# Swapping which half of the split weights takes the recycled slots, and a new order of the first loads, in an attention and rational-gate kernel

## The chip, the cores and the metric

The kernel runs on one core of one Trainium2 chip. The metric is device time in microseconds (us). The engines are PE (matrix products and transposes), DVE, ACT and POOL (elementwise work), and SP, which here only issues DMAs; ACT can issue DMAs too. Each engine takes its instructions in a fixed order and waits at the one whose inputs are not ready.

## The reference

```python
# attention, q k v of shape (4, 8, 768, 64), 8 global keys, a local window of 96
scores = q @ k.T / sqrt(D)  -  slope[h] * distance
scores = where(is_global | is_local, scores, -1e9)
a = softmax(scores)
x = (a @ v)  as (3072, 512)
# feed-forward, w_in (512, 2048), w_out (2048, 512)
h = x @ w_in
P = a[0] + a[1]*h + a[2]*h**2 + a[3]*h**3
Q = 1 + |b[0]|*|h| + |b[1]|*h**2
out = (P / (Q + 1e-6)) @ w_out
```

`moe_w_in` and `moe_w_out` arrive as 64-bit floats. The kernel fetches their raw words and puts them together to 32-bit floats itself.

## The kernel before

**Tiling.** The 3072 rows are 12 chunks of 256 tokens. A chunk has 8 attention units (a unit u is a pair of heads for 128 tokens; 96 units) and 8 feed-forward steps (a step f covers 256 of the 2048 hidden columns; 96 steps). A step's first layer gives h (L277, for chunk 0 L269), a gate of elementwise work follows, and the second layer adds to the chunk's output (L353, for chunk 0 L348). The gate runs over ACT (L301 to L303, logarithm and exponential L317 and L318), DVE (L308, L309, then L322 to L324, whose last instruction ends the gate) and POOL (the sum L310). From chunk 1 on ACT and POOL also split the gate's result into two parts (L332, L333).

**Two kinds of products.** Chunk 0 multiplies in full 32 bits with the decoded weights. From chunk 1 on (step 8), every operand is split into a high part, rounded to the type fp32r, and a low part, the difference; three fp32r products (high by high, high by low, low by high) take the place of one.

**The weights** come in 32 pieces of 128x512: `w_in` piece (1, row block, column block), `w_out` piece (0, row block). `WSCHED` says at which time step which pieces are decoded, beginning with the four of the first column block of `w_in`. A piece is fetched (L177, 512 KB, into one of five raw buffers), decoded on ACT or POOL (L206 to L212) and on DVE (L213, then L215, which ends it) into a full piece, named `w..f`. `first` holds the first five pieces, fetched by `windowed` at the start; each later fetch waits for a raw buffer that a decode leaves. Later `split_w` makes the parts: the copy L228 rounds (DVE and ACT by turns, `HI_V`), the subtraction L229 takes the difference (POOL, from the 14th piece on by turns with DVE, `LO_V`). `SPLITS` sets after which step which pieces are split, in the order of their decoding.

**Places.** High parts lie in two fixed tiles, `win_h` and `wout_h`. Full pieces and low parts share the pool `lows`: 33 slots in rotation. The full pieces come first in it (the first two parts ahead of the last two), so low part n + 1 lands in the slot that full piece n had: the subtraction waits until that piece has been split and read for the last time by chunk 0. The copy writes a fixed place and waits for the decode of its piece alone.

**What sets the order.** Every instruction gets a priority (`tc.cur_priority`, from the time step and the tables `PRI` and `PRI_A`), and a scheduler builds the order of each engine from the priorities, the dependencies and its own times. Splitting (`wsplit`) has the lowest priority, so a copy that is ready is put where an engine would stand idle.

**The start.** SP issues the two flag DMAs (`n_local`, `n_global`, needed by the masks), then q and k of the first units (`st_load(0)`), q and k of the next (`st_load(2)`), V (`st_load_v`), and the remaining fetches. ACT loads its table and issues the first two pieces.

Of the kernel before, what the change touches and what calls it, by code (L numbers as in the profile page):

```python
# [105 lines left out]
def tile_kernel(ctx: ExitStack, tc: tile.TileContext, q, k, v, n_global, n_local,  # L106
# [28 lines left out]
    def st_load(u):  # L135
        c, t, p, b, i = unit(u)
        hs = slice(2 * p, 2 * p + 4)
        r = slice(i * P, (i + 1) * P)
        n = pl.ldp.tile([P, 2, 4, D], F32, tag="nat", name=f"nat{u}")
        nc.sync.dma_start(out=n[:, 0], in_=q[b, hs, r, :].rearrange("h s d -> s h d"))  # L140
        nc.sync.dma_start(out=n[:, 1], in_=k[b, hs, r, :].rearrange("h s d -> s h d"))
        nat[u // 2] = n
# [4 lines left out]
        nc.sync.dma_start(out=vt, in_=v[b, 2 * p:2 * p + 4, i * P:(i + 1) * P, :].rearrange("h s d -> s h d"))  # L147


    win_h = const.tile([P, NCT, DF], FR, name="win_h")  # L150
    wout_h = const.tile([P, NFT, DM], FR, name="wout_h")
    lows = ctx.enter_context(tc.tile_pool(name="lows", bufs=1))
    full = {}
    low = {}

    def piece(dt, key):
        return lows.tile([P, 2 * TOK], dt, tag="w", name=f"w{'_'.join(map(str, key))}{'f' if dt is F32 else 'l'}",
                         bufs=NCT * DF // (2 * TOK) + NFT + 1)

    def w_hi(key):  # L160
        if key[0]:
            return win_h[:, key[1], key[2] * 2 * TOK:(key[2] + 1) * 2 * TOK]
        return wout_h[:, key[1], :]

    def tmp(name):
        return pl.ffn.tile([P, 2, TOK], F32, tag="tmp", name=name, bufs=pl.tmps)
# [57 lines left out]
        return [(0, 2 * n + x) for x in range(2)]  # L224

    def split_w(key):
        low[key] = piece(FR, key)
        (nc.vector.tensor_copy if len(low) - 1 in HI_V else nc.scalar.copy)(out=w_hi(key), in_=full[key])  # L228
        (nc.vector if len(low) - 1 in LO_V else nc.gpsimd).tensor_tensor(  # L229
            out=low[key], in0=full[key], in1=w_hi(key), op=ALU.subtract)  # L230


    gs = {}
# [27 lines left out]
    def st_ffn1(f, y):  # L261
        c, j = divmod(f, FPC)
        if y == 0:
            hps[f] = pl.ps_h.tile(sh, F32, tag="h", name=f"h{f}")
        jw, fw = divmod((2 * j + y) * P, 2 * TOK)
        fs = slice(fw, fw + P)
        if c == 0 and not pl.split:
            for ct in range(NCT):
                nc.tensor.matmul(out=hps[f][:, y, :], lhsT=full[1, ct, jw][:, fs], rhs=xT[c][:, ct, :],  # L269
                                 start=(ct == 0), stop=(ct == NCT - 1))  # L270
            return
        xh, xl = xT[c]
        n = 0
        for ct in range(NCT):
            wh, wl = w_hi((1, ct, jw)), low[1, ct, jw]
            for w, x in ((wh, xh), (wh, xl), (wl, xh)):
                nc.tensor.matmul(out=hps[f][:, y, :], lhsT=w[:, fs], rhs=x[:, ct, :],  # L277
                                 start=(n == 0), stop=(n == 3 * NCT - 1))
                n += 1
# [59 lines left out]
    def st_ffn2(f, t):  # L339
        c, j = divmod(f, FPC)  # L340
        if j == 0:
            accs[c, t] = pl.ps_o.tile([P, DM], F32, tag="acc", name=f"acc{c}_{t}")
        acc = accs[c, t]
        ts = slice(t * P, (t + 1) * P)
        for y in range(2):
            ft = 2 * j + y
            if c == 0 and not pl.split:
                nc.tensor.matmul(out=acc, lhsT=gs[f][:, y, ts], rhs=full[0, ft],  # L348
                                 start=(ft == 0), stop=(ft == NFT - 1))
                continue  # L350
            wh = w_hi((0, ft))
            for n, (z, w) in enumerate(((0, wh), (0, low[0, ft]), (1, wh))):
                nc.tensor.matmul(out=acc, lhsT=gs[f][:, z, y, ts], rhs=w,  # L353
                                 start=(ft == 0 and n == 0), stop=(ft == NFT - 1 and n == 2))
        if j == FPC - 1:
            o = tmp(f"o{c}_{t}").rearrange("p a b -> p (a b)")
            rows = slice(c * TOK + t * P, c * TOK + (t + 1) * P)
            if is_last(f):
                (nc.vector.tensor_copy if t else nc.scalar.copy)(out=o, in_=acc)
            else:  # L360
                nc.any.tensor_copy(out=o, in_=acc)
            nc.sync.dma_start(out=out[rows, :], in_=o)
# [187 lines left out]
    nf = const.tile([P, 4], F32, name="nf")  # L550

    def windowed(lates):
        nc.sync.dma_start(out=ni[:, 0:2], in_=n_local.bitcast(I32).partition_broadcast(P))
        nc.sync.dma_start(out=ni[:, 2:4], in_=n_global.bitcast(I32).partition_broadcast(P))
        first = [key for t in sorted(WSCHED) for kind, j in WSCHED[t] for key in pieces(kind, j)][0:GBUFS + 2]
        scope = ExitStack()
        pl.early = scope.enter_context(tc.tile_pool(name="early", bufs=1))
        pl.kF = pl.early.tile([P, NPAIR, 2, P], F32, name="kF")
        pl.kGF = pl.early.tile([P, NPAIR, G], F32, name="kGF")
        pl.qz = pl.early.tile([P, 3, 2, P], F32, name="qz")  # L560
        nc.scalar.preload_act_table_set("natural_log_exp_and_others")
        st_load(0)
        for n, key in enumerate(first):
            fetch(key, nc.scalar if n < 2 else nc.sync)
            if n == 0:
                st_load(2)
                st_load_v(0)
                st_load_v(2)
        make_identity(nc, ident)
# [244 lines left out]
```

## Time and profile before

| | us |
|---|---|
| median of three runs | 784.45 |
| the three runs | 784.35, 784.45, 787.12 |
| the profiled execution, its own time | 783.55 |
| its span, first to last instruction | 781.5 |
| PE busy | 748.3 |
| granted clock of PE, mean | 0.992 |

All times of the profile are counted from the first instruction. Busy time is the sum over an engine's instructions, overlaps within it taken once; idle time matters only where the engine is what the others wait for. In group names the numbers of buffers are left out: `w_10f` is a full piece, `w_3l` a low part, `nat` holds q and k of two units, `fu` is the operand that the gate gives to the second layer.

### The profile page before, as it was taken

What the parts mean: (1) busy time and instruction counts of PE and PEld (TensorE: products, weight loads), DVE (VectorE), ACT (ScalarE), POOL (GpSimd) and SP (SyncE); (2) the same over time, 40 slices, a digit from 0 to 9 for tenths busy, and PEclk for the clock granted to TensorE, in tenths of its full rate; (3) what the DMA queues carried; (4) which work ended last, traced back from release to release, by engine and by line L of the source; (5) the groups of instructions that cost most, each with busy time, mean ns of one, the idle gap of its engine ahead of it and who ended that gap; (6) DMA issues with size and microseconds to landing.
All of it is one profiled execution on the core that took longest, in us unless ns stands there. A gap on an engine that the chain in (4) does not pass through costs nothing.

```text
span 781.5 us, 15335 instructions
## 1 busy us (share of the span) xinstructions
PE 748.3 (96%) x5216; PEld 648.6 (83%) x5216; DVE 567.6 (73%) x1384; ACT 571.7 (73%) x1404; POOL 501.3 (64%) x548
## 2 busy tenths in 40 slices
PE   3798799999999999999999999999999999999996
PEld 2575466888988988998998998989988989988995
DVE  5899987656677777776776767776776776776665
ACT  4798755876786777877776877777777777776764
POOL 4675785355687686676677676675676677664441
PEclk9999899999999999999999999999999999999999
DMA  8886300202322212222212222222222221100000
GB/s 225 269 265 211 97 16 13 63 22 58 79 49 49 73 44 49 67 51 62 60 43 49 65 52 49 63 56 55 62 48 49 62 56 44 41 22 1 28 1 33
DMA packets 97560, 52.75 MB, mean 68 GB/s; under 512 B 81088, under 2 KB 90304, under 8 KB 97472
## 3 DMA queue, kind: packets, MB, share of 16 engines
q1 hardware_dynamic: 97184, 50.62, 24.6%
q10 hardware_dynamic: 288, 1.05, 0.4%
q8 instruction: 44, 0.72, 0.4%
q14 instruction: 44, 0.36, 0.2%
HBM read 35.92 MB, written 6.29 MB: 54 GB/s over the span
## 4 chain that ended last, share of the span: by engine, by line
PE 88%; DVE 5%; ACT 3%; issue 1%; DMA 1%; POOL 0%; SPq 0%; DVEq 0%; ACTq 0%
PE h L277 33%; PE acc L353 32%; PE o L519 5%; PE s L449 4%; PE tp L497 4%; PE acc L348 3%; PE tk L403 3%; PE h L269 2%; PE s L444 1%; DVE r L213 1%; DMA nat<-in_k_dram 1%; ACT pr L473 1%; PE tk L396 0%; ACT qz L418 0%; DVE w_0f L215 0%
## 5 line engine op out<-in xcount | busy, mean ns | idle before, releaser
L353 PE MATMUL acc<-wout_h,g 128*128 128x512 f32 x704 | 249.3, 405 | 0.0
L277 PE MATMUL h<-xh,win_h 128*128 128x256 f32 x704 | 205.3, 292 | 0.0
L277 PE MATMUL h<-xl,win_h 128*128 128x256 f32 x704 | 197.5, 281 | 0.0
L310 POOL TENSOR_TENSOR fa<-fa,fs 128x512 f32<-128x512 f32 x95 | 124.1, 1306 | 97.1 <-ACT fs L303 93.7
L487 POOL TENSOR_SCALAR pr<-pr,stats 128x256 f32<-128x256 f32 (+1 forms) x152 | 131.4, 875 | 36.9 <-DVE stats L478 26.2
L353 PEld LDWEIGHTS acc<-wout_h,g 128*128 128x128 f32 x704 | 128.8, 188 | 22.0 <-ACT g L332 0.4
L277 PEld LDWEIGHTS h<-xh,win_h 128*128 128x128 f32 x704 | 132.9, 189 | 7.4 <-issue 5.8
L277 PEld LDWEIGHTS h<-xl,win_h 128*128 128x128 f32 x704 | 132.4, 188 | 1.6 <-issue 0.3
L473 ACT ACTIVATE pr<-pr,stats 128x256 f32<-128x256 f32 (+1 forms) x192 | 92.6, 484 | 53.3 <-DVE stats L463 53.2
L333 POOL TENSOR_TENSOR g<-fu,g 128x512 fp32r<-128x512 f32 x87 | 112.6, 1295 | 8.7 <-ACT g L332 6.1
L301 ACT ACTIVATE fu<-h,coef 128x512 f32<-128x512 f32 (+1 forms) x97 | 75.0, 773 | 57.5 <-PE h L277 52.5
L322 DVE SCALAR_TENSOR_TENSOR fu<-fu,coef,q 128x512 f32<-128x512 f32 (+1 forms) x97 | 71.7, 739 | 46.0 <-ACT q L318 45.1
L387 POOL TENSOR_TENSOR sp<-nat,sp 128x256 fp32r<-128x256 f32 x72 | 53.0, 736 | 78.7 <-DVE sp L386 36.7
L317 ACT ACTIVATE fs<-fa,coef 128x512 f32<-128x512 f32 (+1 forms) x97 | 69.6, 717 | 34.3 <-POOL fa L310 33.1
L499 DVE COPY pT<-tp 128x512 f32<-128x512 f32 (+1 forms) x75 | 48.5, 646 | 53.4 <-PE tp L497 52.4
L308 DVE TENSOR_TENSOR fu<-fu,h 128x512 f32<-128x512 f32 (+1 forms) x97 | 65.5, 675 | 19.9 <-ACT fs L303 18.1
L309 DVE SCALAR_TENSOR_TENSOR fu<-fu,coef,h 128x512 f32<-128x512 f32 (+1 forms) x97 | 71.8, 740 | 2.7
L323 DVE SCALAR_TENSOR_TENSOR q<-fa,coef,q 128x512 f32<-128x512 f32 (+1 forms) x97 | 72.1, 743 | 0.0
L463 DVE CUSTOM_DVE_ANT_0 pr<-s,masks 128x256 f32<-128x256 f32 x160 | 61.1, 418 | 11.2 <-PE s L444 5.3
L302 ACT ACTIVATE fa<-h,coef 128x512 f32<-128x512 f32 (+1 forms) x97 | 65.6, 676 | 2.0 <-DVE q L323 1.0
L303 ACT ACTIVATE fs<-h,coef 128x512 f32<-128x512 f32 (+1 forms) x97 | 66.4, 684 | 0.1
L324 DVE SCALAR_TENSOR_TENSOR fu<-q,fu 128x512 f32<-128x512 f32 (+1 forms) x97 | 65.7, 677 | 0.4
(247 smaller groups left out, 1636.3 us busy)
## 6 DMA issues: line engine op xcount, KB each, us to landing
qT<-qT SPq DMA_DIRECT2D x144, 64.0 KB, 2.0
r<-in_moe_w_out_dram SPq DMA_DIRECT2D x16, 512.0 KB, 4.9
r<-in_moe_w_in_dram SPq DMA_DIRECT2D x14, 512.0 KB, 4.6
nat<-in_q_dram SPq DMA_DIRECT2D x48, 128.0 KB, 2.7
nat<-in_k_dram SPq DMA_DIRECT2D x48, 128.0 KB, 2.6
vt<-in_v_dram SPq DMA_DIRECT2D x48, 128.0 KB, 2.4
out_dram<-o SPq DMA_DIRECT2D x24, 256.0 KB, 2.1
r<-in_moe_w_in_dram ACTq DMA_DIRECT2D x2, 512.0 KB, 7.1
```

The costliest lines, as they stand in the source:

```text
L277: nc.tensor.matmul(out=hps[f][:, y, :], lhsT=w[:, fs], rhs=x[:, ct, :], start=(n == 0), stop=(n == 3 * NCT - 1))
L301: nc.scalar.activation(out=u, in_=h, func=AF.Identity, scale=a3, bias=a2)
L303: nc.scalar.activation(out=s, in_=h, func=AF.Square, scale=b1)
L309: nc.vector.scalar_tensor_tensor(out=u, in0=u, scalar=a1, in1=h, op0=ALU.add, op1=ALU.mult)
L310: side(f).tensor_tensor(out=a, in0=a, in1=s, op=ALU.add)
L317: nc.scalar.activation(out=s, in_=a, func=AF.Ln, bias=q1)
L322: nc.vector.scalar_tensor_tensor(out=u, in0=u, scalar=a0, in1=r, op0=ALU.add, op1=ALU.mult)
L323: nc.vector.scalar_tensor_tensor(out=r, in0=a, scalar=q1, in1=r, op0=ALU.add, op1=ALU.mult)
L333: side(f).tensor_tensor(out=g[:, 1, ys], in0=u, in1=g[:, 0, ys], op=ALU.subtract)
L353: nc.tensor.matmul(out=acc, lhsT=gs[f][:, z, y, ts], rhs=w, start=(ft == 0 and n == 0), stop=(ft == NFT - 1 and n == 2))
L473: nc.scalar.activation(out=d, in_=d, func=AF.Exp, scale=-1.0, bias=st[:, x:x + 1], accum_out=st[:, 2 + 2 * x:3 + 2 * x])
L487: nc.gpsimd.tensor_scalar(out=d, in0=d, scalar1=st[:, 6 + x:7 + x], scalar2=None, op0=ALU.mult)
```

## The change

The pool now holds full pieces and high parts (`wide`); the fixed tiles hold the low parts (`win_l`, `wout_l`). Sizes and the rotation stay as they are, and so do all operations and their engines: the copy writes a slot and the subtraction a fixed place. The three products read the same operands from the swapped places.

At the start the two flag DMAs go from SP to ACT, ahead of its table load. SP begins with q and k of the first units, then the first piece, q and k of the next units, the second and third piece, V, and the rest. ACT issues no fetch any more.

```diff
-    win_h = const.tile([P, NCT, DF], FR, name="win_h")
-    wout_h = const.tile([P, NFT, DM], FR, name="wout_h")
-    lows = ctx.enter_context(tc.tile_pool(name="lows", bufs=1))
+    win_l = const.tile([P, NCT, DF], FR, name="win_l")
+    wout_l = const.tile([P, NFT, DM], FR, name="wout_l")
+    wide = ctx.enter_context(tc.tile_pool(name="wide", bufs=1))
...
     def split_w(key):
-        low[key] = piece(FR, key)
-        (nc.vector.tensor_copy if len(low) - 1 in HI_V else nc.scalar.copy)(out=w_hi(key), in_=full[key])
-        (nc.vector if len(low) - 1 in LO_V else nc.gpsimd).tensor_tensor(
-            out=low[key], in0=full[key], in1=w_hi(key), op=ALU.subtract)
+        hi[key] = piece(FR, key)
+        (nc.vector.tensor_copy if len(hi) - 1 in HI_V else nc.scalar.copy)(out=hi[key], in_=full[key])
+        (nc.vector if len(hi) - 1 in LO_V else nc.gpsimd).tensor_tensor(
+            out=w_lo(key), in0=full[key], in1=hi[key], op=ALU.subtract)
...
-            wh, wl = w_hi((1, ct, jw)), low[1, ct, jw]
+            wh, wl = hi[1, ct, jw], w_lo((1, ct, jw))
...
-            wh = w_hi((0, ft))
-            for n, (z, w) in enumerate(((0, wh), (0, low[0, ft]), (1, wh))):
+            wh = hi[0, ft]
+            for n, (z, w) in enumerate(((0, wh), (0, w_lo((0, ft))), (1, wh))):
...
     def windowed(lates):
-        nc.sync.dma_start(out=ni[:, 0:2], in_=n_local.bitcast(I32).partition_broadcast(P))
-        nc.sync.dma_start(out=ni[:, 2:4], in_=n_global.bitcast(I32).partition_broadcast(P))
...
+        nc.scalar.dma_start(out=ni[:, 0:2], in_=n_local.bitcast(I32).partition_broadcast(P))
+        nc.scalar.dma_start(out=ni[:, 2:4], in_=n_global.bitcast(I32).partition_broadcast(P))
+        st_load(0)
         nc.scalar.preload_act_table_set("natural_log_exp_and_others")
-        st_load(0)
         for n, key in enumerate(first):
-            fetch(key, nc.scalar if n < 2 else nc.sync)
-            if n == 0:
+            if n == 1:
                 st_load(2)
+            fetch(key)
+            if n == 2:
                 st_load_v(0)
                 st_load_v(2)
```

The line numbers behind the start move by one.

The first place is SP at the start of the program (`r1_2_0` is the raw buffer of piece (1, 2, 0), `vt` holds V). Before, where two pieces more stand on ACT's queue:

```order
L553 DMA ni_69<-in_n_local_dram 128x2
L554 DMA ni_69<-in_n_global_dram 128x2
L140 DMA nat0_101<-in_q_dram 128x4x64
L141 DMA nat0_101<-in_k_dram 128x4x64
L140 DMA nat2_106<-in_q_dram 128x4x64
L141 DMA nat2_106<-in_k_dram 128x4x64
L147 DMA vt0_109<-in_v_dram 128x4x64
L147 DMA vt2_111<-in_v_dram 128x4x64
L177 DMA r1_0_0_115<-in_moe_w_in_dram 128x1024
L177 DMA r1_1_0_117<-in_moe_w_in_dram 128x1024
L177 DMA r1_2_1_119<-in_moe_w_in_dram 128x1024
```

And now:

```order
L140 DMA nat0_100<-in_q_dram 128x4x64
L141 DMA nat0_100<-in_k_dram 128x4x64
L177 DMA r1_2_0_104<-in_moe_w_in_dram 128x1024
L140 DMA nat2_106<-in_q_dram 128x4x64
L141 DMA nat2_106<-in_k_dram 128x4x64
L177 DMA r1_3_0_109<-in_moe_w_in_dram 128x1024
L177 DMA r1_0_0_111<-in_moe_w_in_dram 128x1024
L147 DMA vt0_113<-in_v_dram 128x4x64
L147 DMA vt2_115<-in_v_dram 128x4x64
L177 DMA r1_1_0_117<-in_moe_w_in_dram 128x1024
L177 DMA r1_2_1_119<-in_moe_w_in_dram 128x1024
```

q and k of the first units have moved to the front of SP, the first two pieces have joined it, and V has moved behind the third piece.

The second place is DVE near the end of the decoding, around the last instruction of step 2's gate (L324 with `fu2`; the ISA rows are the masked scores of L463). Before:

```order
L308 TENSOR_TENSOR fu3_811<-fu3_811,h3_793 128x512
L215 SCALAR_TENSOR_TENSOR w0_11f_931<-w0_11f_931,r0_11_932 128x512
L463 ISA pr14_942,stats_64<-s14_938,masks_68 128x256
L463 ISA stats_64 128x1
L463 ISA pr14_942,stats_64<-s14_938,masks_68 128x256
L463 ISA stats_64 128x1
L546 TENSOR_TENSOR xl1_675<-o5_834,xh1_674 128x2x128
L228 CAST wout_h_59<-w0_10f_924 128x512
L215 SCALAR_TENSOR_TENSOR w0_13f_1016<-w0_13f_1016,r0_13_1017 128x512
L213 SCALAR_TENSOR_TENSOR r0_14_1087<-r0_14_1087 128x512
L324 SCALAR_TENSOR_TENSOR fu2_729<-q2_804,fu2_729 128x512
L228 CAST wout_h_59<-w0_12f_1009 128x512
```

And now, where the copy L228 that follows is the first one on DVE:

```order
L213 SCALAR_TENSOR_TENSOR r0_12_1010<-r0_12_1010 128x512
L215 SCALAR_TENSOR_TENSOR w1_3_3f_860<-w1_3_3f_860,r1_3_3_861 128x512
L476 TENSOR_REDUCE stats_64<-stats_64 128x2
L546 TENSOR_TENSOR xl1_675<-o5_834,xh1_674 128x2x128
L324 SCALAR_TENSOR_TENSOR fu2_729<-q2_804,fu2_729 128x512
L213 SCALAR_TENSOR_TENSOR r0_11_932<-r0_11_932 128x512
L215 SCALAR_TENSOR_TENSOR w0_10f_924<-w0_10f_924,r0_10_925 128x512
L309 SCALAR_TENSOR_TENSOR fu3_811<-fu3_811,coef_63,h3_793 128x512
L228 CAST w1_2_0h_1023<-w1_2_0f_174 128x512
L215 SCALAR_TENSOR_TENSOR w0_12f_1009<-w0_12f_1009,r0_12_1010 128x512
L213 SCALAR_TENSOR_TENSOR r0_13_1017<-r0_13_1017 128x512
L478 RECIPROCAL stats_64<-stats_64 128x2
```

Before, fourteen copies of DVE stand ahead of this L324; now none does, and the last steps of the decodes of `w0_10` to `w0_13` stand behind it.

The third place is POOL where the first layer of chunk 1 gets its weights (L229 writes the low part; the gate's sum L310 between them belongs to steps 4 to 7). Before, a subtraction reads a full piece and the fixed tile, and writes a slot:

```order
L229 TENSOR_TENSOR w1_2_1l_1177<-w1_2_1f_272,win_h_58 128x512
L229 TENSOR_TENSOR w1_3_1l_1180<-w1_3_1f_277,win_h_58 128x512
L310 TENSOR_TENSOR fa4_902<-fa4_902,fs4_903 128x512
L229 TENSOR_TENSOR w1_0_1l_1183<-w1_0_1f_310,win_h_58 128x512
L229 TENSOR_TENSOR w1_1_1l_1186<-w1_1_1f_317,win_h_58 128x512
L229 TENSOR_TENSOR w0_0l_1262<-w0_0f_386,wout_h_59 128x512
L229 TENSOR_TENSOR w0_1l_1265<-w0_1f_393,wout_h_59 128x512
```

And now it reads a full piece and the slot of its high part:

```order
L229 TENSOR_TENSOR win_l_58<-w1_2_1f_272,w1_2_1h_1177 128x512
L229 TENSOR_TENSOR win_l_58<-w1_3_1f_277,w1_3_1h_1180 128x512
L451 COPY kF_95<-kGF_96 128x8
L229 TENSOR_TENSOR win_l_58<-w1_0_1f_310,w1_0_1h_1183 128x512
L310 TENSOR_TENSOR fa6_1064<-fa6_1064,fs6_1065 128x512
L229 TENSOR_TENSOR win_l_58<-w1_1_1f_317,w1_1_1h_1186 128x512
L229 TENSOR_TENSOR wout_l_59<-w0_0f_386,w0_0h_1262 128x512
L229 TENSOR_TENSOR wout_l_59<-w0_1f_393,w0_1h_1265 128x512
```

The same subtractions stand about one and a half steps later among the gates' sums. Copy n + 1 writes the slot of full piece n, which subtraction n reads, so before each subtraction a copy on DVE or ACT has to have run that waited for the subtraction before it.

More of the change, by code (lines that the diff above doesn't have):

```diff
@@ L147, in st_load_v, with w_lo @@
         nc.sync.dma_start(out=vt, in_=v[b, 2 * p:2 * p + 4, i * P:(i + 1) * P, :].rearrange("h s d -> s h d"))
-    win_h = const.tile([P, NCT, DF], FR, name="win_h")
-    wout_h = const.tile([P, NFT, DM], FR, name="wout_h")
-    lows = ctx.enter_context(tc.tile_pool(name="lows", bufs=1))
+    win_l = const.tile([P, NCT, DF], FR, name="win_l")
+    wout_l = const.tile([P, NFT, DM], FR, name="wout_l")
+    wide = ctx.enter_context(tc.tile_pool(name="wide", bufs=1))
     full = {}
-    low = {}
+    hi = {}
     def piece(dt, key):
-        return lows.tile([P, 2 * TOK], dt, tag="w", name=f"w{'_'.join(map(str, key))}{'f' if dt is F32 else 'l'}",
+        return wide.tile([P, 2 * TOK], dt, tag="w", name=f"w{'_'.join(map(str, key))}{'f' if dt is F32 else 'h'}",
                          bufs=NCT * DF // (2 * TOK) + NFT + 1)
-    def w_hi(key):
+    def w_lo(key):
         if key[0]:
-            return win_h[:, key[1], key[2] * 2 * TOK:(key[2] + 1) * 2 * TOK]
-        return wout_h[:, key[1], :]
+            return win_l[:, key[1], key[2] * 2 * TOK:(key[2] + 1) * 2 * TOK]
+        return wout_l[:, key[1], :]
     def tmp(name):
```

## The prediction

> **What bounds the kernel now.** I read the page first: busy times, and the 40 slices of 19.5 us.
>
> ```profile
> PE 748.3 (96%) x5216; PEld 648.6 (83%) x5216; DVE 567.6 (73%) x1384; ACT 571.7 (73%) x1404; POOL 501.3 (64%) x548
> ...
> PE   3798799999999999999999999999999999999996
> ...
> DVE  5899987656677777776776767776776776776665
> ```
>
> PE is the bound of the whole, but not of the first five slices, where DVE has the nines. The busy time by stages sets the borders (columns: stretch, its length, then busy us of each engine, granted clock, DMA share, GB/s).
>
> ```profile
> 0.00:10.00 10.00, 0.45 (x1) 0.18 (x1) 2.52 (x13) 2.50 (x3) 3.39 (x16) 1.00 0.64 161
> 10.00:30.00 20.00, 15.57 (x76) 11.37 (x76) 17.29 (x65) 13.74 (x55) 9.46 (x13) 0.91 1.00 296
> 30.00:95.00 65.00, 52.68 (x299) 37.64 (x297) 64.00 (x137) 55.70 (x141) 47.16 (x49) 0.96 0.67 205
> 95.00:140.00 45.00, 44.79 (x217) 30.31 (x217) 35.52 (x72) 25.57 (x61) 30.94 (x26) 0.98 0.08 19
> 140.00:188.00 48.00, 48.00 (x342) 41.11 (x341) 30.95 (x74) 36.86 (x86) 24.19 (x23) 1.00 0.17 42
> 188.00:775.00 587.00, 586.81 (x4289) 527.98 (x4286) 416.77 (x1027) 437.12 (x1061) 386.18 (x423) 1.00 0.20 48
> ```
>
> From 95 us to 775 us PE idles 0.4 us, and the change leaves its matmuls as they are. So time can be won only from PE's idle 26.3 us before 95 us (9.6 in the first 10, 4.4 up to 30, 12.3 up to 95), and lost anywhere behind. Before 10 us everybody waits for the first transfers; from 10 to 30 us the DMA share is 1.00; from 30 to 95 us DVE is busy 64 of 65 us and PE waits for it.
>
> **The change part by part. First, the rounding copies (L228).** Before, they write a fixed place and run as soon as a piece is decoded. Now a copy writes into a slot that an older piece must leave first, and on DVE all 16 stand behind the end of step 2's gate, which 14 of them stood ahead of. L228 alone, by stage (DVE, then ACT):
>
> ```profile
> 0.00:30.00 30.00, 2.03 (x4) 1.24 (x2) 0.94 0.88 251
> 30.00:95.00 65.00, 6.36 (x10) 7.96 (x13) 0.96 0.67 205
> 95.00:105.00 10.00, 1.96 (x2) 0.62 (x1) 0.90 0.00 1
> ```
>
> In the stretch where DVE is the bound, ten copies with 6.36 us leave DVE, and thirteen with 7.96 us leave ACT (55.70 of 65 us busy, so second in line). Not all of it is on the path. In the chain of waits from 30 to 95 us L228 has eight pieces, 4.85 us together (start, length), of which first, longest and last are:
>
> ```profile
> 30.52 0.35 ACT win_h L228
> ...
> 71.94 1.43 DVE wout_h L228
> ...
> 91.88 0.39 DVE wout_h L228
> ```
>
> Bounds: 0 us (if another engine takes the same time there) and 6.36 us. I take the chain's own figure, **4.8 us**. The 2.03 us before 30 us I count at nothing: the DMA rate covers them.
>
> **Second, the order behind the copies.** Step 2's gate ends (L324) at 94.47 us, and PE's first unbroken stretch waits for it. Ahead of it on DVE stand the second halves of four decodes (L215) that now stand behind it:
>
> ```profile
> 84.19 1.75 DVE L215 SCALAR_TENSOR_TENSOR w_10f<-w_10f,r 128x512 int32<-128x512 int32 x1
> ...
> 88.86 0.68 DVE L215 SCALAR_TENSOR_TENSOR w_12f<-w_12f,r 128x512 int32<-128x512 int32 x1
> ...
> 90.12 0.74 DVE L215 SCALAR_TENSOR_TENSOR w_11f<-w_11f,r 128x512 int32<-128x512 int32 x1
> ...
> 92.20 1.75 DVE L215 SCALAR_TENSOR_TENSOR w_13f<-w_13f,r 128x512 int32<-128x512 int32 x1
> ...
> 94.47 0.68 DVE L324 SCALAR_TENSOR_TENSOR fu<-q,fu 128x512 f32<-128x512 f32 x1
> ```
>
> That is 1.75 + 0.68 + 0.74 + 1.75 = 4.9 us. It is moved, not saved: the next gate (step 3) has all four ahead of it as before, so PE may run into a second gap. Bounds 0 and 4.9 us; I take **2.0 us**, nearer to nothing.
>
> **Third, the start.** Before, k of the first units is issued at 2.12 us and lands 7.88 us later, while two weight pieces load from ACT's queue; PE starts with it. The flags land for DVE at 7.79 us, the first piece for ACT at 7.36 us.
>
> ```profile
> 2.12 7.88 DMA nat<-in_k_dram
> ...
> 10.05 0.49 PE tk L396
> ...
> 1.19 0.41 SPq L554 DMA_DIRECT2D ni<-in_n_global_dram  x1
> ...
> 7.36 0.66 ACT L208 ACTIVATE w_0f<-r 128x512 f32<-128x512 f32 x1 [5.35 <-DMA r<-in_moe_w_in_dram]
> ...
> 7.79 0.17 DVE L573 CAST nf<-ni 128x4 f32<-128x4 int32 x1 [5.14 <-DMA ni<-in_n_global_dram]
> ...
> nat<-in_k_dram SPq DMA_DIRECT2D x48, 128.0 KB, 2.6
> ```
>
> Now q and k are SP's first two DMAs, and the pieces stand behind them on the same queue. Issued second, at about 1.2 us as the second flag was, k lands between 3.8 us (the median 2.6 us) and 9.1 us (again 7.88 us); I take 4.5 us, 5.5 us earlier, since no weights run beside it. ACT carries the two flag DMAs ahead of its table load; what then waits on ACT is the first units' q and k, which come later anyway. SP carries two fetches more, and V behind the third piece; V's first reader comes after the first probabilities, so I cost both at nothing; if V came late, the first units' product would wait, inside the same start.
>
> PE's 5.5 us are not the kernel's. DVE can move its masks forward by up to 7.79 - 4 = 3.8 us, but the next 20 us run at a DMA share of 1.00 with the same bytes, which holds the decodes where they were. Bounds 0 and 5.5 us; I take **2.5 us**.
>
> The Trainium skill, in DMA: Bandwidth & Descriptors, section "Issuing engines are not separate DMA queues", says that DMAs of all engines run on the same 16 DMA engines and interleave, and that another issuing engine saves only the time of issuing. By that rule moving two pieces from ACT to SP gives nothing by itself, and what is left is the order; taken at its word, with the stretch from 10 to 30 us full, the third term would be 0 and the sum 2.5 us smaller. The 7.88 us against the median of 2.6 us bear out the interleaving; no run yet shows the order's worth.
>
> **Fourth, what is added later.** The splits become one chain: copy n waits for the subtraction n - 1 (it writes the slot that one read), and subtraction n waits for copy n. Before, only the subtractions formed a chain. The copies leave the first 95 us for the time up to about 180 us, beside PE at 100%. What a link costs is read from:
>
> ```profile
> L229 POOL TENSOR_TENSOR w_3l<-w_3f,win_h x2: 1267/1270/1272, 123.0 to 126.1; 128x512 fp32r<-128x512 f32 x2
> L229 DVE TENSOR_TENSOR w_3l<-w_3f,win_h x2: 693/872/1050, 125.0 to 127.4; 128x512 fp32r<-128x512 f32 x2
> ...
> L228 ACT CAST win_h<-w_2f x2: 619/620/620, 45.7 to 53.7; 128x512 fp32r<-128x512 f32 x2
> ...
> L228 DVE CAST wout_h<-w_2f x1: 406/406/406, 43.6 to 43.6; 128x512 fp32r<-128x512 f32 x1
> ...
> L228 DVE CAST wout_h<-w_8f x1: 1516/1516/1516, 71.9 to 71.9; 128x512 fp32r<-128x512 f32 x1
> ```
>
> With POOL a link is about 1.27 + 0.41 to 0.62, some 1.9 us with no queue; with DVE 0.69 + 0.62, some 1.3 us; plus what stands ahead in each queue, an estimate of 1 us. Copies and subtractions that wait hold up what is behind them: on DVE the gates (L308 to L324), on ACT the exponentials, on POOL the sums (L310), and PE waits for the gates. Room for it: from 95 to 188 us DVE is busy 66.5 of 93 us, ACT 62.4, POOL 55.1. Fourteen more copies at 0.41 us are 5.7 us on DVE, at 1.52 us (the worst row) 21 us; ACT gets 9 us. Both fit into the idle time at the low price, and at the high one almost all of DVE's 26.5 us is gone. Bounds 0 and 6 us of PE time; I take **1.0 us**.
>
> In the Trainium skill, SBUF — State Buffer, section "Who interferes with whom", a DVE copy in its two-port mode and a GpSimd instruction exclude each other for the whole instruction. The trace agrees in kind: the same copy takes 0.41 us or 1.52 us. By that rule the copies now stand where POOL subtracts, and the fourth term would go to its upper end; against it, each copy waits for a subtraction that has just left POOL.
>
> **The sum.** 4.8 + 2.0 + 2.5 - 1.0 = 8.3 us off the profiled execution, which took 783.55 us (span 781.5 and 2.05 us around it): 775.25 us. The median of the three runs is 784.45 us, 0.9 us above that execution; from it the sum gives 776.15 us. I predict **775.7 us**.
>
> **Rivals.**
>
> More is won (767 to 772.5 us). If DVE alone holds the stretch up to 95 us, all of 6.36 + 4.9 and 3.8 us come out, 15 us: 768.5 us. For it speaks 64.00 of 65 us; against it that ACT is on the chain too, and that PE's idle cannot fall below what the first transfers leave.
>
> The decodes are held by something else (779 to 782 us). The pieces come no faster because DMA share 1.00 up to 30 us and five raw buffers set their pace, and the idle only moves to another releaser; or q and k do not land earlier, and the change doesn't do what it says there. Then 2 to 4 us are left: 780.5 us. Against it: DMA share 0.67 from 30 to 95 us.
>
> The gain is eaten (780.5 to 785 us). The added copies and in-order waits make DVE or ACT the bound in the first steps with split weights, 140 to 188 us. ACT has 36.86 of 48 us there; six steps' copies are some 4 us, and waits can take the rest. Price 6 us of PE time: 783.55 - 9.3 + 6 = 780.3 us, and up to 785 us where the first three terms bring only half.
>
> **Slower: the split chain starves PE.** The tightest use is step 14's first layer, which needs the 26th piece. Before, it is read by ACT at 179.95 us:
>
> ```profile
> 179.95 0.78 ACT L301 ACTIVATE fu<-h,coef 128x512 f32<-128x512 f32 x1 [1.79 <-PE h L277]
> ```
>
> and starts some 4 us earlier; 8 us less makes 168 us. The chain begins where the first subtraction stood:
>
> ```profile
> 82.12 3.27 POOL L229 TENSOR_TENSOR w_0l<-w_0f,win_h 128x512 fp32r<-128x512 f32 x2
> ```
>
> at 82.12 us before, so at 74 us now, and 26 links have 94 us, 3.6 us each; my estimate of a link is 1.3 to 1.9 us plus 1 us of queues, so 2.3 to 2.9 us. From 3.6 us on PE waits; at 4.2 us it waits 26 x 0.6 = 16 us, and the time is 783.55 - 9.3 + 16 = 790 us. Against it: two thirds of the budget, and in the instruction order the 26th subtraction stands three steps ahead of its reader.
>
> **How the numbers follow.** Forecast (772.5 to 779 us) 0.45; more is won 0.15; decodes held by something else 0.18; gain eaten 0.12; chain starves PE 0.10. A measurement of this kernel tells about 0.5% from no change, 3.9 us. Below 780.5 us lie the first two and nearly half of the third: 0.68 faster. Within 3.9 us lie the rest of the third and the fourth: 0.22. Slower is the last: 0.10. The range leaves out the slower case and the outermost part of "more is won": 767 to 783 us; the terms' lower bounds (0 + 0 + 0 - 6) reach beyond it.
>
> **What the profile of the changed kernel would show.** First term: L228 with no DVE time before about 75 us, and PE's unbroken stretch beginning near 87 us. Second: step 2's L324 earlier by more than step 3's. Third: the first transpose of PE near 5 us, the flags' cast near 4 us. Fourth: PE idle 95 to 188 us of at most about 1 us, and the last L229 before 170 us. I am wrong if PE's idle before its unbroken stretch stays above 22 us, or if PE waits for L229 or for a gate behind it.

## The result, and the profile after

The changed kernel took **776.23 us** (median of four runs, 773.83 to 777.12) beside 785.09 us of the kernel before on the same chip (784.35 to 787.12): ratio 0.9878, 95% interval 0.9848 to 0.9908, about 9 us less. The prediction was 775.7 us. The profiled execution took 773.83 us with a span of 771.9 us, 9.6 us less than the span before. The sum was right; its first two terms together were too small, the third was too large, and the errors cancelled, so that its nearness to the result is in part luck.

The page's 40 slices of the changed kernel: PE's low digits are gone after the third slice.

```profile
PE   5779999999999999999999999999999999999996
...
DVE  5899976986777776676677777667776677776665
```

The same stages as before (stretch, its length, busy us of PE, PEld, DVE, ACT and POOL, granted clock, DMA share, GB/s):

```profile
0.00:10.00 10.00, 2.24 (x8) 1.61 (x8) 2.76 (x20) 3.30 (x7) 2.59 (x16) 1.00 0.62 186
10.00:30.00 20.00, 14.96 (x83) 10.79 (x82) 15.89 (x59) 14.58 (x59) 10.88 (x13) 1.00 0.99 282
30.00:95.00 65.00, 57.91 (x334) 42.39 (x332) 62.09 (x133) 51.00 (x129) 47.58 (x48) 0.97 0.66 206
95.00:140.00 45.00, 45.00 (x248) 32.30 (x247) 32.92 (x81) 34.39 (x82) 26.85 (x25) 1.00 0.12 32
140.00:188.00 48.00, 48.00 (x335) 41.32 (x334) 39.19 (x82) 36.05 (x89) 35.43 (x30) 1.00 0.17 38
```

PE's idle time before 95 us is 7.8 + 5.0 + 7.1 = 19.9 us; it was 26.3. That is 6.4 of the 9.6 us. The other 3.6 us are busy time: PE is busy for 744.7 us instead of 748.3 with the same matmuls (behind 95 us it idles 0.4 us more than before). The last section comes back to that.

The copies (L228) by stage, DVE and then ACT: nothing on DVE before 84 us, and from then on the same copies beside a busy PE.

```profile
0.00:30.00 30.00, 0.00 (x0) 0.00 (x0) 1.00 0.86 250
30.00:84.00 54.00, 0.00 (x0) 0.41 (x1) 0.97 0.72 224
84.00:95.00 11.00, 1.25 (x2) 0.19 (x2) 1.00 0.37 117
95.00:105.00 10.00, 0.83 (x2) 1.22 (x2) 1.00 0.11 25
105.00:200.00 95.00, 6.99 (x12) 8.05 (x13) 1.00 0.18 42
```

From the timeline, the gates of steps 2 and 3 (the start of their last instruction, L324). Before, step 2's stood at 94.47 us and step 3's here:

```profile
103.98 0.68 DVE L324 SCALAR_TENSOR_TENSOR fu<-q,fu 128x512 f32<-128x512 f32 x1
```

So they come 11.8 and 10.3 us earlier. From 57 to 95 us PE now idles 1.3 us (36.72 of 38 busy); 0.97 us of it are the wait for step 3's gate.

```profile
82.68 0.68 DVE L324 SCALAR_TENSOR_TENSOR fu<-q,fu 128x512 f32<-128x512 f32 x1
...
93.69 0.68 DVE L324 SCALAR_TENSOR_TENSOR fu<-q,fu 128x512 f32<-128x512 f32 x1
...
94.42 1.13 PE L348 MATMUL acc<-w_6f,fu 128*128 128x512 f32 x2 [0.97 <-DVE fu L324]
```

The start, again from the timeline (in brackets the idle time ahead of an instruction, and what ended it), first PE's first matmul before, then the changed kernel:

```profile
9.54 0.99 PE L396 MATMUL tk<-ident,nat 128*128 128x128 f32 x2 [9.54 <-DMA nat<-in_q_dram]
```

```profile
4.03 0.45 PE L396 MATMUL tk<-ident,nat 128*128 128x128 f32 x1 [4.03 <-DMA nat<-in_q_dram]
5.92 0.17 DVE L574 CAST nf<-ni 128x4 f32<-128x4 int32 x1 [3.26 <-DMA ni<-in_n_global_dram]
7.27 0.48 PE L396 MATMUL tk<-ident,nat 128*128 128x128 f32 x1 [2.79 <-DMA nat<-in_k_dram]
7.78 0.57 ACT L418 ACTIVATE qz<-tk 64x128 f32<-64x128 f32 x2 [4.83 <-PE tk L396]
...
8.62 0.67 ACT L208 ACTIVATE w_0f<-r 128x512 f32<-128x512 f32 x1
```

PE begins at 4.0 us instead of about 9.5, but the first piece's decode on ACT begins 1.3 us later than before (7.36 us). It shows no wait of its own: in ACT's order it now stands behind the copies of the first units' q and k (L418 to L422), and ACT waits 4.83 us for these.

### The profile page after: what moved, and what is told of

It reads as the page before. It is cut to its first block, busy times and chain, and to the rows that moved or that the text cites. A ratio compares the mean times of both kernels' runs of the same rounds, so it can differ in the third digit from the quotient of the medians.

```text
span 771.9 us, 15342 instructions
## 1 busy us (share of the span) xinstructions
PE 744.7 (96%) x5216; PEld 647.8 (84%) x5216; DVE 563.4 (73%) x1384; ACT 570.7 (74%) x1404; POOL 504.5 (65%) x548
## 4 chain that ended last, share of the span: by engine, by line
PE 86%; DVE 6%; DMA 2%; issue 2%; POOL 1%; ACT 1%; SPq 0%; DVEq 0%; POOLq 0%; ACTq 0%
PE h L277 33%; PE acc L353 32%; PE o L519 5%; PE tp L497 4%; PE s L449 4%; PE tk L403 3%; PE acc L348 2%; DVE r L213 2%; PE s L444 2%; PE h L269 1%; DMA nat<-in_k_dram 1%; DVE pr L463 1%; DMA r<-in_moe_w_in_dram 1%; DMA out_dram<-o 1%; DMA r<-in_moe_w_out_dram 0%
## 5 line engine op out<-in xcount | busy, mean ns | idle before, releaser
L277 PE MATMUL h<-xh,win_l 128*128 128x256 f32 x704 | 197.7, 281 | 0.0
L310 POOL TENSOR_TENSOR fa<-fa,fs 128x512 f32<-128x512 f32 x95 | 124.8, 1314 | 92.8 <-ACT fs L303 86.7
L353 PE MATMUL acc<-wout_l,g 128*128 128x512 f32 x352 | 139.4, 396 | 0.0
L277 PEld LDWEIGHTS h<-xh,win_l 128*128 128x128 f32 x704 | 133.1, 189 | 0.9 <-issue 0.3
L353 PEld LDWEIGHTS acc<-wout_l,g 128*128 128x128 f32 x352 | 66.3, 188 | 9.6
L324 DVE SCALAR_TENSOR_TENSOR fu<-q,fu 128x512 f32<-128x512 f32 (+1 forms) x97 | 65.7, 678 | 0.4
L332 ACT CAST g<-fu 128x512 fp32r<-128x512 f32 (+1 forms) x89 | 55.5, 624 | 12.1 <-DVE fu L324 12.0
L463 DVE CUSTOM_DVE_ANT_0 pr<-s,masks 128x256 f32<-128x256 f32 x160 | 61.1, 418 | 3.7 <-PE s L444 2.2
L497 PE MATMUL tp<-ident,pr 128*128 128x128 f32 x352 | 59.4, 275 | 2.5 <-DVE stats L463 2.3
```

Source lines behind the costliest of these rows:

```text
L310: side(f).tensor_tensor(out=a, in0=a, in1=s, op=ALU.add)
L353: nc.tensor.matmul(out=acc, lhsT=gs[f][:, z, y, ts], rhs=w, start=(ft == 0 and n == 0), stop=(ft == NFT - 1 and n == 2))
L497: nc.tensor.transpose(out=t_ps[:, x, w, :], in_=pr[:, x, w, :], identity=ident)
```

## The experiments

The theory to test: the copies leave the stretch in which DVE (and behind it ACT) sets the pace, and that this is all of the gain. The rivals: the start, the order of the decodes at the gate, or late costs that hide a larger gain. All ratios are to the kernel before, run beside them on the same chip (medians 785.1 to 786.1 us); PE's busy time before 95 us is from one profiled execution.

| run | us, median | ratio, 95% interval | PE busy before 95 us | gates of steps 2 and 3, us |
|---|---|---|---|---|
| before | 786.06 | 1 | 68.69 | 94.47, 103.98 |
| changed kernel | 776.23 | 0.9878, 0.9848 to 0.9908 | 75.11 | 82.68, 93.69 |
| places alone | 775.89 | 0.9878, 0.9853 to 0.9903 | 75.41 | 85.52, 95.20 |
| start alone | 785.71 | 0.9999, 0.9982 to 1.0016 | 69.82 | 100.36, 109.10 |
| old places, copies held | 781.73 | 0.9943, 0.9923 to 0.9964 | 74.74 | 81.87, 93.08 |
| early copies back on both | 784.96 | 0.9982, 0.9967 to 0.9997 | 71.61 | 96.05, 106.94 |
| back on DVE | 783.26 | 0.9963, 0.9947 to 0.9979 | 74.04 | 90.63, 105.05 |
| back on ACT | 779.56 | 0.9916, 0.9894 to 0.9938 | 73.29 | 90.59, 101.36 |
| subtraction twice | 795.31 | 1.0126, 1.0105 to 1.0147 | 75.29 | 84.18, 95.94 |
| subtraction three times | 840.17 | 1.0697, 1.0671 to 1.0722 | 74.63 | 83.28, 95.32 |
| two pieces from ACT's queue | 780.18 | 0.9920, 0.9894 to 0.9947 | 70.67 | 89.58, 98.99 |
| mixed start | 779.47 | 0.9910, 0.9892 to 0.9929 | 70.80 | 87.54, 95.92 |
| late decodes, new start | 781.96 | 0.9946, 0.9926 to 0.9966 | 73.95 | 85.71, 98.66 |
| late decodes, old start | 779.61 | 0.9925, 0.9904 to 0.9946 | 73.97 | 86.31, 98.48 |

**The two halves of the change.** The first run has the new places (`split_w`, `piece`, `w_lo`) and the start of before (the lines of `windowed` taken back); the second the reverse.

> The new places of the high and low parts alone, with the start of the kernel before. Theory A (the places carry nearly all of it: the copies leave the stretch from 30 to 95 us; the start gives little, since by 30 us the changed kernel's PE had only 1.2 us more of busy time): about 777.5 us, 7.5 us under the kernel before, and step 2's gate (L324) ends near 84 us. Rival B (the terms of the prediction, 2.5 us of the gain from the start): 779.3 us. Rival C (the start costs as much as it brings, because the first piece is decoded later): 776.2 us or less, as fast as the changed kernel or faster.

> The new start alone, with the old places. Theory A: about 783.7 us, 1.4 us under the kernel before, and the stretch from 30 to 95 us keeps its idle PE time of about 12 us. Rival B: 782.6 us. Rival C: 785 us or more. In all three the copies (L228) stand in the first 95 us as before.

Measured: the places alone give the whole gain, 1.22%; the start alone gives 0.0%, and on top of the places nothing either. That is rival C: the start costs what it brings. The stages up to 95 us, of the places alone and then of the start alone:

```profile
0.00:10.00 10.00, 0.35 (x1) 0.18 (x1) 2.33 (x13) 2.49 (x3) 3.28 (x16) 1.00 0.62 160
10.00:30.00 20.00, 15.18 (x74) 11.29 (x73) 17.02 (x61) 13.49 (x54) 11.80 (x14) 0.91 1.05 306
30.00:95.00 65.00, 59.89 (x328) 42.18 (x326) 63.16 (x138) 52.30 (x133) 45.86 (x49) 0.97 0.66 202
```

```profile
0.00:10.00 10.00, 2.14 (x7) 1.58 (x8) 2.71 (x19) 3.28 (x7) 2.59 (x16) 1.00 0.61 178
10.00:30.00 20.00, 15.72 (x76) 11.09 (x75) 15.62 (x59) 13.54 (x54) 9.38 (x10) 0.83 0.98 279
30.00:95.00 65.00, 51.96 (x290) 37.81 (x290) 62.25 (x132) 53.35 (x137) 48.16 (x48) 0.95 0.68 207
```

The new start brings PE 1.8 us of work forward before 10 us, but DVE has 17.02 us of work in the next 20 us with the old start and 15.62 with the new one. The second decoded piece on DVE (L215), before and changed, suggests why: its last step begins 3.7 us later.

```profile
13.13 0.68 DVE L215 SCALAR_TENSOR_TENSOR w_0f<-w_0f,r 128x512 int32<-128x512 int32 x1
```

```profile
16.84 2.19 DVE L215 SCALAR_TENSOR_TENSOR w_0f<-w_0f,r 128x512 int32<-128x512 int32 x2
```

PE's early start is spent in a stretch where PE is not the bound; DVE, which is the bound later, starts behind. This is read from the traces; no run tried the one without the other.

**Is it the places, or only when the copies run?** Old places and old start, each copy held until its slot is free:

```diff
         low[key] = piece(FR, key)
+        cp = nc.vector.tensor_copy if len(low) - 1 in HI_V else nc.scalar.copy
+        cp(out=low[key][:, 0:1], in_=full[key][:, 0:1])
+        cp(out=w_hi(key)[:, 0:1], in_=low[key][:, 0:1])
```

> Places and start of the kernel before, but each rounding copy is held until its piece's slot for the low part is free: two copies of one column, through that slot, go ahead of it on its engine (64 small instructions more). Theory A (what counts is only when the copies run): the time of the places alone, 777.5 us, plus up to 1.5 us for the small instructions. Rival D (the new places themselves matter, or the order of the code): near the kernel before, 784 to 786 us.

Measured: neither number. Up to 95 us it is the kernel with the new places (gates at 81.87 and 93.08 us, PE busy for 74.74 us), so it is enough to run the copies late; up to there the places as such add nothing that shows. Then it loses time that the theory had not counted. PE's waits between 130 and 780 us (here L231 is the copy):

```profile
PE h L280 <- DVE win_h L231: 1.2, 1, 1.2
PE h L280 <- ACT win_h L231: 0.9, 2, 0.7
PE acc L356 <- DVE wout_h L231: 0.6, 1, 0.6
```

The two small instructions lengthen each link of the split chain: 32 links from 82.59 us (start of the first subtraction) to 211.32 us (end of the last) are 4.02 us each, against 2.69 us in the changed kernel (84.27 to 170.20). PE now waits for the chain: from 95 to 300 us it idles 3.4 us, where with the new places alone it idles none. That is about half of the 6.5 us by which this profiled execution is longer than that of the places alone (spans of 780.0 and 773.5 us); 2.4 us more are PE's busy time, which no row explains. The run was meant to test the first term and also tested the fourth.

**Which engine's copies?** The changed kernel with the early copies put back, as dead work into the fixed place, on both engines, on DVE (`n in HI_V`) or on ACT (the others):

```diff
+        n = len(hi)
         hi[key] = piece(FR, key)
+        if n in HI_V:
+            (nc.vector.tensor_copy if n in HI_V else nc.scalar.copy)(out=w_lo(key), in_=full[key])
```

> The changed kernel, with the early copies put back beside the late ones: each piece is also copied into the fixed place of its low part as soon as it is decoded (dead work; the subtraction overwrites it). Theory A (the early copies are what the change takes away, and the late ones cost nothing): 782 to 784.5 us, step 2's gate near 93 us, PE without idle time from 95 to 188 us. Rival E (the late copies' cost was hidden in the result, or the gain comes from elsewhere): under 779 us, or above 786 us.

> The changed kernel with the early copies put back on DVE alone (16 of the 32; dead work). In its order step 2's gate (L324) stands ahead of the four late decodes, as in the changed kernel, so only the time of the copies on DVE comes back. Theory A1 (DVE's time is what counted, 6 to 7 us of copies before 95 us): 781 to 783 us. Rival A2 (the order of the four decodes counted as much as the time): 778 to 780 us. Rival A3 (ACT's copies counted): under 778 us.

> The changed kernel with the early copies put back on ACT alone (the other 16; dead work). DVE has no early copies, but in its order three of the four late decodes stand ahead of step 2's gate again. Theory A1 (DVE's time): 776 to 778 us, nearly the changed kernel. Rival A2 (the order): 778 to 780 us. Rival A3 (ACT's copies): 781 us or more.

Measured: both give back 1.04% (8.2 us of 786), DVE's alone 0.85% (6.7 us), ACT's alone 0.38% (3.0 us). The two add up to 1.23%, as much as the gain; run together they cost less, and 0.18% (1.4 us, interval 0.03 to 0.33%) stays won, for which no run shows the cause. With DVE's alone, ten copies stand between 30 and 95 us again:

```profile
30.00:95.00 65.00, 7.92 (x10) 0.92 0.68 202
```

DVE's copies cost nearly what they last. The theory's number for DVE alone was slightly too low (783.26 us, expected 781 to 783). With ACT's alone, thirteen copies with 8.04 us stand there, and the run is not "nearly the changed kernel". But 779.56 us is the number of rival A2, which put it on the order of the decodes: this run has three of the late decodes ahead of step 2's gate, and so has the run with two pieces from ACT's queue, further down, which loses as much (0.9920) without any early copy. So the 3.0 us are not shown to be the price of ACT's copies.

Much of what comes back is busy time of PE and not idle time. With both, the span of the profiled execution is 11.3 us longer than the changed kernel's, 7.8 of them in PE's busy time; with DVE's alone 9.8 and 6.0; with ACT's alone 5.8 and 4.5. The last section has a part of the reason.

With DVE's copies back the instruction order keeps step 2's gate ahead of the four late decodes, as in the changed kernel. Its gates in the timeline of that run (line 327 here):

```profile
90.63 0.68 DVE L327 SCALAR_TENSOR_TENSOR fu<-q,fu 128x512 f32<-128x512 f32 x1
...
105.05 0.68 DVE L327 SCALAR_TENSOR_TENSOR fu<-q,fu 128x512 f32<-128x512 f32 x1
```

Step 2's gate is 3.8 us earlier than before and step 3's 1.1 us later: what stood ahead of the one now stands ahead of the other. In this pair of runs the order is moved, not saved.

**How near is the split chain to starving PE?** The changed kernel with each subtraction done twice, and three times (`for _ in range(2)`, `range(3)` ahead of the subtraction in `split_w`; the subtraction is then line 230).

> The changed kernel with each subtraction of the split (L229) done three times (dead work on the same engine), so that a link of the chain grows by 2.5 us with POOL and 1.4 us with DVE, on the mean of 32 links (22 on POOL, 10 on DVE) by 2.2 us, from 2.65 to about 4.8 us. Theory (the chain of the splits has a budget of some 3.6 us a link, and beyond it PE waits): 26 links are late by 26 x 1.2 = 31 us where nothing gives way, less where the queues ahead of a link overlap with it; PE waits 10 to 30 us for L228, L229 or the gates behind them between 100 and 250 us, and the time is 785 to 806 us. Rival (the chain has slack, and POOL and DVE hide the work): under 779 us.

> The changed kernel with each subtraction of the split (L229) done twice (dead work on the same engine). With three the chain took about 6 us a link and the kernel 840 us; with one it takes 2.65 us and PE never waits. Theory (PE waits from about 3.6 us a link): a link lands between, at 3.7 to 4.3 us, and PE waits 2 to 15 us for the split chain and the gates and sums behind it: 779 to 793 us. Rival (the budget is larger, 4.5 us or more): no wait of PE for the chain, 776 to 778 us.

The chain's first and last subtraction, changed kernel and then three times:

```profile
84.27 1.75 POOL L229 TENSOR_TENSOR win_l<-w_0f,w_0h 128x512 fp32r<-128x512 f32 x1 [0.52 <-ACT w_0h L228]
...
169.53 0.67 DVE L229 TENSOR_TENSOR wout_l<-w_15f,w_15h 128x512 fp32r<-128x512 f32 x1
```

```profile
84.37 1.32 POOL L230 TENSOR_TENSOR win_l<-w_0f,w_0h 128x512 fp32r<-128x512 f32 x1 [0.89 <-ACT w_0h L228]
...
280.01 3.28 DVE L230 TENSOR_TENSOR wout_l<-w_15f,w_15h 128x512 fp32r<-128x512 f32 x3
```

And PE's waits between 95 and 300 us with three subtractions (total, how often, longest):

```profile
PE tk L404 <- POOL sp L388: 9.0, 7, 3.8
PE acc L354 <- POOL wout_l L230: 8.3, 4, 5.2
PE h L278 <- POOL win_l L230: 5.1, 2, 2.8
```

The largest of them in the run with two subtractions:

```profile
PE tk L404 <- POOL sp L388: 6.2, 6, 2.1
```

Measured: PE starves, as in the slower rival of the prediction. A link of 2.69 us (changed kernel) leaves PE 0.25 us idle between 95 and 300 us, 4.02 us (copies held) 3.4 us, 4.65 us (twice) 14.3 us, 6.22 us (three times) 41.1 us. The line through the last two has a slope of (41.1 - 14.3) / 1.57 = 17 us per us of link and meets zero at 3.8 us; at 4.02 us it gives 3.6, where 3.4 was measured on another kernel. The 3.8 us are an estimate from this line, and not of the chain alone: with two subtractions the waits of PE for the chain itself (copies and subtractions) are 4.1 of the 14.3 us, and the largest one is for the operands of q and k, which POOL's longer work delays. What the runs bound is this: at 2.69 us a link PE does not wait for the chain, at 4.02 us it does, with POOL's work unchanged. Both times lie above what was expected (840 us against at most 806, 795 against at most 793), because the links came out longer: 6.2 us instead of 4.8, and 4.65 instead of at most 4.3. PE's clock also falls around its waits (mean 0.967 over the run with three), so the time grows by more than PE's idle time. With the measured links the prediction's own formula, 26 links times the excess over 3.6 us on top of 774.25 us, gives 774.25 + 26 x 1.05 = 801.6 us and 774.25 + 26 x 2.62 = 842.4 us: a little high at the first and near at the second. That nearness is partly luck: the formula puts all 68 us of the second on PE's waiting, but PE idles 41.1 us there, and its busy time grows by 24 us (768.9 instead of 744.7).

**Other starts and a later schedule.** The first keeps the changed start but lets ACT issue the first two pieces; the second lets ACT issue them ahead of everything and puts the third piece ahead of the second q and k; two more have the last twelve decodes due one to two steps later (`WSCHED`), with the new and the old start.

```diff
-            fetch(key)
+            fetch(key, nc.scalar if n < 2 else nc.sync)
```

```diff
-          10: [(0, 2)], 11: [(0, 3)], 12: [(0, 4), (1, 6)], 13: [(1, 7)], 14: [(0, 5)], 15: [(0, 6)], 16: [(0, 7)]}
+          11: [(0, 2)], 12: [(0, 3)], 13: [(0, 4), (1, 6)], 14: [(1, 7)], 16: [(0, 5)], 17: [(0, 6)], 18: [(0, 7)]}
```

> The changed kernel with its first two pieces issued by ACT instead of SP, each at its place in the code of the start. The instruction order that follows has three of the four late decodes ahead of step 2's gate on DVE (the changed kernel: none). Theory F (the issuing engine gives nothing, the order of the decodes at the gate counts): 778 to 780 us, as with the ACT copies put back and as with the mixed start, both near 779.5 us. Rival G (neither counts): 775.5 to 777 us. Rival H (the second queue gets the first pieces to ACT and DVE earlier): under 775 us.

> The changed kernel with a start that takes from both: the first two pieces on ACT's queue at once (as in the kernel before), the flags behind them, q and k of the first unit first on SP's queue, the third piece ahead of the second pair's q and k. Theory (until 30 us the transfers' rate decides, after it DVE; no order of the same bytes is worth much): 775 to 777 us, no difference from the changed kernel that can be measured. Rival (the first piece's landing sets DVE's lead, and q and k set PE's): 773 to 774.5 us, better than both kernels.

> The changed kernel with the decodes of the last twelve pieces due one to two steps later in the schedule, so that less of them stands ahead of the first gates (none ahead of step 2's as in the changed kernel, two fewer ahead of step 3's, and copies ahead of the gates instead). Theory (what leaves DVE before 95 us is won nearly in full): 1 to 3 us under the changed kernel, 773 to 775 us. Rival (DVE takes whatever is ready, so the same work stands there in another order): 775.5 to 777.5 us.

> The new places with the start of the kernel before, and the later schedule of the last twelve decodes as in the run before this one. Theory: 1 to 3 us under the places alone, 773 to 775 us. Rival: 775 to 777.5 us.

Measured: all four have ratios 0.3 to 0.7% above the changed kernel's, but only that of the late decodes with the new start lies clear of its interval; the other three touch it. By their medians the other two starts lose 3 to 4 us, although one of them decodes its first piece 3.4 us earlier than the changed kernel. The first decode on ACT, two pieces from ACT's queue and then mixed start:

```profile
9.56 0.67 ACT L208 ACTIVATE w_0f<-r 128x512 f32<-128x512 f32 x1
```

```profile
5.18 0.66 ACT L208 ACTIVATE w_0f<-r 128x512 f32<-128x512 f32 x1 [1.10 <-DMA r<-in_moe_w_in_dram]
```

The landing of the first piece alone does not explain it, and the order at step 2's gate does not either: in both runs already step 0's gate comes 3.5 to 3.8 us later than in the changed kernel (67.22 and 66.95 against 63.44 us). Among what differs ahead of it is when other first loads arrive. With two pieces from ACT's queue k lands at 8.2 us (changed kernel: 7.2) and the flags' cast on DVE runs at 7.4 us (5.9); with the mixed start it runs only at 11.2 us:

```profile
11.22 0.41 DVE L576 CAST nf<-ni 128x4 f32<-128x4 int32 x1 [3.02 <-DMA ni<-in_n_global_dram]
```

No run moved these loads alone. Two pieces from ACT's queue came out just above theory F's range (780.18 us), but its reason is not shown; the mixed start missed both of its numbers (779.47 us). The later schedule missed both of its numbers as well, and its expectation misread its order: with the new start one decode (w_10f) and two copies stand ahead of step 2's gate, where the changed kernel has neither, and four copies instead of two ahead of step 3's. DVE took what was ready, as the rival said, and L228 had 2.98 us between 30 and 95 us instead of 1.25; both times are worse than even the rival's. So the position of the four decodes at the gate does not tell the time by itself; what sets the differences of 3 to 6 us among these orders is open. No run beat the changed kernel; the places alone equal it.

## Why the prediction held, and where not

**The bound.** Right: PE's idle time before 95 us held the win, and DVE set the pace there; what ACT added is open. PE's unbroken stretch, forecast from 87 us on, begins at 57.2 us but for the 0.97 us at step 3's gate. Next to nothing was lost behind 95 us. What it did not see is that PE's busy time changes too: 3.6 of the 9.6 us.

**First term, copies leave the early stretch (4.8 us).** The mechanism was right: late copies bring the early part of the gain even in the old places, and early copies give back 8.2 us. The term was mis-sized. It counted the copies' pieces on one chain of waits (2.75 us of DVE and 2.1 of ACT) and took DVE's own 6.36 us as the upper bound. The runs put DVE's copies at 6.7 us and both at 8.2. The upper bound was too small: it left out ACT's copies, although the chain had four pieces of ACT, and it counted no busy time of PE; how much either adds stays open.

**Second term, order at step 2's gate (2.0 us).** Its signature came, weakly: step 2's gate is earlier by 11.8 us and step 3's by 10.3, and PE has a second, short gap there (0.97 us at step 3's gate). With DVE's copies back in the same order, nothing of the 2 us is left at step 3, which speaks for the lower bound of 0 and for the sentence "moved, not saved". But the two runs with three of the decodes ahead of the gate lose 3 to 4 us for whatever reason, and the places alone, with one decode ahead of it, lose nothing. The term stays open.

**Third term, the start (2.5 us).** Wrong; measured 0.1 us with an interval from -1.3 to 1.4. The step that failed: "which holds the decodes where they were". The decodes did not stay. The first begins 1.3 us later on ACT, behind the first units' q and k; the prediction had "what then waits on ACT is the first units' q and k, which come later anyway" and did not see that a decode waits with them. The second piece, now behind q and k on SP's queue, reaches POOL 2.0 us later (before, then changed), and its last step on DVE begins 3.7 us later. k landed at 7.2 us instead of the 4.5 forecast, and the flags' cast came at 5.9 us instead of 4.

```profile
8.90 1.51 POOL L206 TENSOR_SCALAR w_0f<-r 128x512 f32<-128x512 f32 x1 [0.25 <-DMA r<-in_moe_w_in_dram]
```

```profile
10.94 1.71 POOL L206 TENSOR_SCALAR w_0f<-r 128x512 f32<-128x512 f32 x1 [3.18 <-DMA r<-in_moe_w_in_dram]
```

The sentence on the Trainium skill (DMA: Bandwidth & Descriptors, section "Issuing engines are not separate DMA queues") gave 0 us for this term, and for the changed start that is what the runs show. That an issuing engine makes no difference they do not show: with two pieces from ACT's queue the kernel is 0.4% slower by its median, k lands 1.0 us later, and the first decode, again behind q and k on ACT, begins 0.9 us later. Its instruction order differs too, so the issuing engine is not singled out.

**Fourth term, late cost (1.0 us).** Within its bounds, at the lower end: PE idles 0.0 us from 95 to 188 us, and the last subtraction ends at 170.2 us, 0.2 us behind the forecast. The link was estimated at 2.3 to 2.9 us and measured 2.69; the budget was put at 3.6 us, and the runs leave it between 2.69 and 4.02. The rule of SBUF — State Buffer (section "Who interferes with whom") in the Trainium skill, by which this term would go to its upper end, did not decide: nine of DVE's sixteen copies took 0.41 to 0.43 us, the other seven were longer, the worst 1.40 us, and PE did not wait for it. Two groups of the changed kernel's copies (min/median/max in ns):

```profile
L228 DVE CAST w_2h<-w_2f x3: 426/427/428, 113.3 to 121.4; 128x512 fp32r<-128x512 f32 x3
...
L228 DVE CAST w_10h<-w_10f x1: 1397/1397/1397, 152.0 to 152.0; 128x512 fp32r<-128x512 f32 x1
```

**The sum.** Terms one and two were 2.8 us too small for what the places brought (6.8 against 9.6), the third 2.5 us too large, the fourth 1 us too large as a cost. The range and the sign followed from the bound, not from the terms; that the total came within 1 us is luck.

## What to carry to other kernels

Work that leaves a stretch can be worth nearly its duration on the engine that bounds that stretch, and a second busy engine may add to it; put it back one engine at a time, and look at the instruction order before you call the difference a price, since here other orders alone moved the median by 3 to 6 us. An engine that starts earlier won nothing here, where the engine that bounds the next stretch started later for it. A chain through a rotating buffer cost nothing here while a link was well below its budget (work ahead of the reader divided by links) and then many times the excess, so compute the link and the budget before adding a wait.

## What the runs showed of the hardware

PE's clock can make idle time cost more than its length. Behind some of PE's waits the granted clock falls to 0.50 for 3 to 10 us, and matmuls take about twice as long. From the kernel before, two pairs of matmuls of one kind, the first pair in a slow slice:

```profile
95.21 1.97 PE L348 MATMUL acc<-w_4f,fu 128*128 128x512 f32 x2 [0.48 <-DVE fu L324]
97.01 1.02 PE L348 MATMUL acc<-w_5f,fu 128*128 128x512 f32 x2
```

Also from the kernel before (a matmul with the wait ahead of it, then two slices of 2 us with PE's busy time first and the granted clock third from the end), and from the changed kernel:

```profile
91.60 0.69 PE L514 MATMUL o<-ident,stats 128*64 128x128 f32 x4 [4.72 <-DVE stats L463]
```

```profile
26.00:28.00 2.00, 1.98 (x16) 1.58 (x15) 1.93 (x6) 1.51 (x6) 0.83 (x2) 0.50 0.86 316
...
92.00:94.00 2.00, 2.00 (x8) 1.41 (x5) 2.00 (x3) 1.09 (x6) 1.33 (x1) 0.50 0.00 0
```

```profile
57.17 5.41 PE L269 MATMUL h<-x,w_1f 128*128 128x256 f32 x16 [2.22 <-DVE fu L309]
```

```profile
58.00:60.00 2.00, 2.00 (x6) 1.62 (x5) 2.00 (x7) 1.91 (x5) 1.92 (x2) 0.50 0.33 76
```

Busy time times the clock that was missing, over such slices up to 140 us, is 4.0 us before and 1.7 us after: 2.3 of the 3.6 us of busy time that the change saved; the other 1.3 us have no row. In the run of the start alone it was 10.1 us, in a profiled execution whose span was 787.7 us, the longest among the kernels without added work. With the early copies back on both engines it was 7.4 us, on DVE 4.4 and on ACT 6.4. The Trainium skill, in TensorE: Matmul & The Clock Gate, section "HAM oscillation — how this bites in real kernels", warns of idle gaps above about 3.4 us. The 4.72 us agree; but here the clock also fell behind a gap of 2.22 us, and the slow slices from 24 to 30 us follow waits of only 1.3 us. The length of the gap alone does not decide: behind this one of the kernel before the clock stayed at 1.00.

```profile
77.40 0.66 PE L497 MATMUL tp<-ident,pr 128*128 128x128 f32 x4 [2.16 <-ACT kF L420]
```

The clock goes with the scatter between executions of the kernel before (783.7 to 789.15 us in 24 of them): the 13 with a mean granted clock of 0.990 or more have a median of 785.03 us, the 10 with 0.988 or less one of 787.56 us. Whether the clock is the cause or waits are the cause of both was not tried.
